# All of f on ScalarE's queue, the chain to the row of sums in two column pieces, and a new order of operations

## The chip, the cores and the metric

The kernel runs on one core of one Trainium2 chip. The metric is device time in microseconds (us), the median of several runs. All times in this document are us unless a unit stands beside them.

## The reference

An attention with a forget gate is followed by a bilinear feed-forward layer. There are 8 batches, 8 heads, 576 positions and 64 columns a head; the layer has 4608 tokens, 512 model columns and 1536 inner columns.

```python
scores = scale * np.matmul(q, k.transpose(0, 1, 3, 2))
log_f = np.log(np.clip(f, 0.0001, 1.0))
cum = np.cumsum(log_f, axis=-1)
decay = cum[:, :, :, None] - cum[:, :, None, :]
scores = np.where(causal, -1000000000.0, scores + decay)
...
attn = attn / (np.sum(attn, axis=-1, keepdims=True) + 1e-09)
x = np.matmul(attn, v)            # then heads side by side: 4608 x 512
out = (x @ w_a) * (x @ w_b) @ w_out
```

`f` has one number for each batch, head and position. In a row of scores the term of the query's own position is the same for all keys and falls out in the softmax, so the kernel needs only the running sum of -log f over the keys.

## The kernel before

**Tiles.** A tile t is a batch b and a pair of heads (t = 4b + pr, 32 tiles). Its 576 queries are cut into five blocks i = 0 to 4 of 128 (the last of 64) and its scores into groups: group 0 holds the blocks 1 and 0, group 1 block 2 (384 keys wide), group 2 block 3, group 3 block 4. A group's scores are made in PSUM by `qk_group` (L390), the row maximum is taken on VectorE (`do_max`, L474, for batch 0; `do_decay`, L500, which also adds the sums, for the others), the exponential on ScalarE (`do_exp`, L531 and L527), the reciprocal of its sum on VectorE (L541, L539), the product with it on GpSimd (`do_norm`, L549). The probabilities are turned either by TensorE (batch 0, `pe_tr`, L569) or by a DMA transpose of the SP queue (`do_tr`, L563), and multiplied with v (`do_pv` L591, `do_pv4` L607). The attention's result lies turned in `xT`. Tiles of batch 0 and 1 have their turned probabilities in the unused second half of `xT` (the tiles `xT0` to `xT3` in a DMA's name), later ones in `PTA` and `PTB`. The feed-forward layer makes `psa` and `psb` (`ff_mm`, L861), copies and multiplies them (L213 on ScalarE, L872 on VectorE, giving `ht`), and makes `pso` (L881).

**The opening.** f is loaded in four DMAs of 32 partitions each: two from ScalarE's queue (`f_load`, `f_rows`, L173), two from GpSimd's. Then comes a chain with one instruction a step over all 576 columns: VectorE clips (L184), ScalarE takes the logarithm (L186), VectorE makes the running sum (L187), its upper half in 16 bits (L189) and, in partitions of its own, the rest (L190). The result is `crow`, 128 partitions of 576 sums in fp16. TensorE adds it to the scores of batch 0 (a matmul `sc<-crow,pick` in `qk_group`) and spreads it over partitions for batch 1 (`spread_mm`, L442, tile `scd`). The sums also go to memory (L195) and come back as `spread` for the later batches (L453). Meanwhile q and k of batch 0 come in by four loads of the SP queue (L243: q, k, and a second half of each, which lies in the tile `wout`), are made fp16 (`cast_qk`, L211 to L217, on any of three engines), turned on TensorE (`pe_transpose`, L258, tile `psT`) and copied to `qT` and `kT` (`pe_evict`). ScalarE loads a table for the logarithm and one for the exponential; `warm_table` (L176) does it ahead of time with one small activation each.

**The order.** Every operation is an `Op` with engines that may do it. Two lists made beforehand, `ORDER` (the numbers of all operations in the order of their issue) and `CHOICE` (a letter for each operation that several engines may do: D VectorE, A ScalarE, P GpSimd), decide everything; `laid_out` reads them. Each engine works strictly in the order in which its instructions were issued, and so do the DMA queues: an instruction that waits holds up all behind it on its engine. The costs and due times in `Op` (durations, `prio`, `land`) served to find the lists and do nothing at run time.

**Buffers.** Two score buffers (`sc`), three of `ff` in PSUM (for `psT`, `scd`, `psP`, `psa`, `psb`, `pso`), one of `pv`.

Of the kernel before, what the change touches and what calls it, by code (L numbers as in the profile page):

```python
# [11 lines left out]
EXP = mybir.ActivationFunctionType.Exp  # L12
# [13 lines left out]
def kernel(  # L26
# [138 lines left out]
    def f_load(_):  # L165
        f_rows(nc.scalar, 0)

    def f_rows(eng, c):
        if not cw:
            f_tiles()  # L170
        rows = f.rearrange("b (h p) s -> h b p s", h=2)
        for half in range(2):
            eng.dma_start(out=cw["f"][64 * half + 32 * c:64 * half + 32 * c + 32, :], in_=rows[half])  # L173

    def warm_table(func):
        return lambda _: nc.scalar.activation(out=warm, in_=warm, func=func)  # L176
# [7 lines left out]
    o1 = Op("DVE", 0.45, lambda _: nc.vector.tensor_scalar(out=cw["f"], in0=cw["f"], scalar1=1e-4,  # L184
                                                           scalar2=1.0, op0=MAX, op1=MIN), [o_f, o_f2], prio=-300)
    o2 = Op("ACT", 0.7, lambda _: nc.scalar.activation(out=cw["l"], in_=cw["f"], func=LN), [o1, o_w], prio=-300)  # L186
    o3 = Op("DVE", 1.35, lambda _: nc.vector.tensor_tensor_scan(  # L187
        out=cw["f"], data0=cw["1"], data1=cw["l"], initial=0.0, op0=MUL, op1=SUB), [o2, o0], prio=-300)
    o4 = Op("DVE", 0.45, lambda _: nc.vector.tensor_copy(out=cw["h"], in_=cw["f"]), [o3], prio=-300)  # L189
    o5 = Op("DVE", 0.75, lambda _: nc.vector.scalar_tensor_tensor(  # L190
        out=crow, in0=cw["h"], scalar=lowrow[:, 0:1], in1=cw["f"], op0=MUL, op1=ADD), [o4, o_c], prio=-300)
# [4 lines left out]

    o6 = Op("SP", 1.1, cum_store, [o3], prio=-300, land=0.4)
    o_e = Op("ACT", 1.4, warm_table(EXP), [o2], prio=-300)
    for u in s_users:
        u.extend([o_f2, o0, o1, o2, o3, o4, o5, o6])  # L200
# [437 lines left out]
    def attention(t, base):  # L638
# [12 lines left out]
        if not direct:  # L651
            if t in PSPREAD:
# [3 lines left out]
                for h in range(2):  # L656
                    bm = Op("PE", 512 * COLS, lambda _, h=h: spread_mm(t, h), [o5, bc0] + bcs, prio=prio(0) - 5, mode="full", name=f"bm{t}")
# [15 lines left out]
        for gs in ([(0,), (1,), (2, 3)] if b in EARLY else [(0, 1), (2, 3)]):  # L673
            deps = [kq_ops[(w, b, pr)] for w in "qk"] + [o_c] + ([o5] if direct else bcs)
# [285 lines left out]
    for n in cuts:  # L960
# [3 lines left out]
        0 1 3 4 19 13 25 31 2 37 20 5 21 6 14 22 7 23 15 26 12 16 260 8 24 11 17 9 54 32 27 18 261 57 28 63 33  # L964
        30 58 262 65 29 59 64 55 263 34 69-71 36 99 264 60 66 35 102 38 39 41 234 10 144 103 108 110 109 104 40
# [3 lines left out]
        56 175 138 220 75 139 81 221 176 183 184 207 87 76-78 241 228 82 229 88 83 242 101 243 118 163 80 79 164  # L969
# [8 lines left out]
        384 385 460 470 301 467 468 289 386 290 296 297 469 291 292 232 1676-1678 479 317 298 1679 374 410 411  # L978
# [4 lines left out]
        1702 1704 420 1703 432 433 428 427 429 1705-1707 421 1708 306 307 1709 399 417 439 440 435 434 1710-1713  # L983
        446 447 441 482 1714 1716 358 1718 1715 442 1719 1720 422 1717 443 489 448 1722-1724 1721 491 498 359
        492 1725 499 505 506 1726 1728 1730 356 1727 493 500 449 357 1729 501 502 436 394 395 400 424 444 431
        430 527 423 445 450 494 490 512 1731 507 508 1732 513 483 488 1733 517 509 484 402 403 655 451 453
        1734-1736 518 495 514 519 520 1739 529 454 1740 531 455 521 532 545 538 539 546 510 438 437 511 497
        503 504 496 522 523 533 1737 1741 1744 1746 408 650 566 452 530 1742 534 1745 540 541 1747 515 516 409
        406 1748 542 535 552 553 547 548 1749-1754 1756 1757 554 537 656 528 536 549 550 544 407 524 1755 557
        1758 1759 485 567 651 551 543 1760-1762 558 555 1763-1765 559 560 1766 1767 657 525 569 1743 608 662 676  # L990
        667 658 1768 659 1769 570 573 1770 1771 456 580 561 457 587 574 581 588 571 652 1772 458 562 556 563-565
        1738 575 653 654 1774 1776 1773 582 576 1777 583 459 1775 1778 572 1780 1779 590 1781 1782 584 577 594
        1783 1784 1786 589 1785 1788-1790 595 1787 596 663 579 568 591 1791 599 600 609 593 585 586 592 668 578
        602 1792-1794 664 1795 601 666 611 615 603 597 598 665 629 616 613 623 617 605 604 660 718 1796 661 677
        719 618 1797-1799 630 622 1800 612 619 1802 625 1803 632 624 631 606 607 674 672 1804 1805 614 636 637
        633 1806 1808 1807 1809 1810 638 1811 610 641 1812 626 1813-1815 642 635 621 634 628 675 620 627 643
# [4 lines left out]
        740 726 1850-1852 741 735 734 728 1853 742 724 746 747 846 760 856 850 761 720 751 752 847 802 848 748  # L1001
        1855-1857 851 717 716 1801 763 753 852 754 861 1854 854 743 729 749 736 1858 730 738 744 737 731 750 767
        769 768 775 770 853 781 755 774 776 777 745 857 757 771 782 765 758 1860-1862 783-785 766 1865 788 789
# [57 lines left out]
        2315 2314 2317 2316 2319 2318 2321 2320 2322 2323 2326 2324 2327 2325 2328 2331 2329 2332-2334 2330 2335  # L1061
# [49 lines left out]
```

## Time and profile before

| | us |
|---|---|
| runs | 417.01, 418.45, 418.51 |
| median | 418.45 |
| the profiled execution | 415.86 |
| its span, first to last instruction | 414.1 |
| TensorE busy | 391.0 (94%) |
| VectorE busy | 301.3 (73%) |
| ScalarE busy | 276.9 (67%) |
| GpSimd busy | 254.7 (62%) |

The profile is of one execution, 1.76 longer than its span and 2.59 below the median of the runs. PE is TensorE, DVE VectorE, ACT ScalarE, POOL GpSimd; "SPq" and "ACTq" are the sequencers that issue DMAs. A row of the timeline has the start, the duration, the engine, the line of the kernel, the tile written and those read, the shapes, and in brackets how long the engine had been idle before and what ended the wait. A matmul's end is modelled and overlaps with the next one's start, so for TensorE the distance of two starts counts.

### The profile page before, as it was taken

The page shows a single profiled execution, that of the slowest core. Times are in us where ns is not written, and L with a number is a line of the kernel's source. Part 1 is how long each engine was busy: PE and PEld are TensorE (multiplying, and loading weights), DVE is VectorE, ACT ScalarE, POOL GpSimd, SP SyncE. Part 2 cuts the span into 40 slices and gives each one's busy share as a digit, 9 for nine tenths or more (in the row PEclk, how much of TensorE's full clock was granted, in tenths as well). Part 3 has the DMA queues.
Part 4 walks back from the last instruction along what each step waited for, and adds up shares of the span by engine and source line. Part 5 has one row for each costly group of instructions (what it writes and reads, how often), then busy time and mean ns, then how long its engine had stood idle before and what let it go on. Part 6 is the DMA issues. An engine that isn't in the chain of part 4 may idle for free.

```text
span 414.1 us, 10945 instructions
## 1 busy us (share of the span) xinstructions
PE 391.0 (94%) x3860; PEld 212.0 (51%) x3860; DVE 301.3 (73%) x1002; ACT 276.9 (67%) x788; POOL 254.7 (62%) x442
## 2 busy tenths in 40 slices
PE   0688999998999999999999999999999999999996
PEld 0445785765755544444444544454444444444552
DVE  2889998996878958867987889678777885342240
ACT  2786899775867797766777687687787583231231
POOL 8699698766876867674886687676675745000000
PEclk9999999998999999999999999999999999999999
DMA  8899799999999999999979999999689727300202
GB/s 272 175 220 258 172 210 228 236 206 268 294 239 218 286 229 192 267 215 281 192 206 249 237 271 220 246 211 244 170 181 221 185 57 145 116 1 2 101 2 77
DMA packets 153528, 80.72 MB, mean 195 GB/s; under 512 B 130784, under 2 KB 133344, under 8 KB 153472
## 3 DMA queue, kind: packets, MB, share of 16 engines
q1 hardware_dynamic: 149536, 75.01, 77.1%
q0 software_dynamic: 3856, 4.87, 7.0%
q8 instruction: 30, 0.49, 0.5%
q14 instruction: 26, 0.21, 0.2%
q10 hardware_dynamic: 80, 0.15, 0.1%
HBM read 52.20 MB, written 9.58 MB: 149 GB/s over the span
## 4 chain that ended last, share of the span: by engine, by line
PE 82%; ACT 5%; DVE 4%; DMA 4%; POOL 2%; issue 1%; SPq 1%; POOLq 0%; DVEq 0%; ACTq 0%
PE psa L861 22%; PE pso L881 21%; PE psb L861 21%; PE sc L390 9%; PE pv L591 5%; ACT PA L531 2%; PE psT L258 2%; DMA wout<-in_k_dram 2%; DVE st L474 1%; DMA xT<-PA 1%; PE psP L569 1%; DVE S L500 1%; ACT PB L531 1%; PE sc L607 1%; SPq L563 1%
## 5 line engine op out<-in xcount | busy, mean ns | idle before, releaser
L500 DVE CUSTOM_DVE_ANT_0 S<-sc,spread 64x576 f32<-64x576 f32 (+4 forms) x232 | 125.3, 561 | 8.3 <-PE sc L390 3.5
L861 PE MATMUL psa<-xT,wa 128*128 128x512 f16 (+2 forms) x528 | 115.8, 342 | 0.9 <-DVE ht L872 0.5
L861 PE MATMUL psb<-xT,wb 128*128 128x512 f16 (+2 forms) x528 | 115.6, 342 | 0.3 <-ACT PTB L213 0.3
L549 POOL TENSOR_SCALAR PA<-PA,st 128x128 f16<-128x128 f16 (+2 forms) x192 | 90.1, 483 | 21.0 <-DVE st L541 13.9
L872 DVE TENSOR_TENSOR ht<-psb,a 128x512 f16<-128x512 f32 (+2 forms) x132 | 77.7, 590 | 34.8 <-PE psb L861 28.3
L213 ACT CAST a<-psa 128x512 f16<-128x512 f32 (+2 forms) x132 | 66.4, 504 | 53.4 <-PE psa L861 46.6
L881 PE MATMUL pso<-wout,ht 128*128 128x512 f16 x432 | 99.0, 382 | 0.4 <-DVE osb L217 0.4
L531 ACT ACTIVATE PA<-S,st 128x256 f16<-128x256 f32 (+2 forms) x168 | 84.2, 505 | 12.6 <-DVE st L500 12.5
L549 POOL TENSOR_SCALAR PB<-PB,st 128x512 f16<-128x512 f16 (+1 forms) x96 | 67.8, 715 | 28.1 <-DVE st L541 12.0
L861 PEld LDWEIGHTS <-wb 128*128 128x128 f16 x528 | 50.8, 98 | 40.8 <-issue 0.4
L861 PEld LDWEIGHTS <-wa 128*128 128x128 f16 x528 | 49.0, 98 | 41.3 <-issue 2.6
L881 PEld LDWEIGHTS <-ht 128*128 128x128 f16 x432 | 40.9, 98 | 47.7 <-issue 1.1
L531 ACT ACTIVATE PB<-S,st 128x512 f16<-128x512 f32 x56 | 40.2, 719 | 13.6 <-DVE st L500 12.4
L390 PE MATMUL sc<-kT,qT 64*128 64x128 f16 (+5 forms) x480 | 43.8, 278 | 3.9 <-ACT PA L531 2.2
L531 ACT ACTIVATION_READ_ACCUMULATOR PA<-S,st 128x1 f32 x168 | 32.3, 192 | 0.0
L390 PEld LDWEIGHTS <-qT 64*128 64x128 f16 (+1 forms) x480 | 17.3, 97 | 26.7 <-issue 20.8
L527 ACT ACTIVATE PB<-S,st 128x576 f16<-128x576 f32 x28 | 21.7, 776 | 12.3 <-issue 5.4
L541 DVE RECIPROCAL st<-st 128x2 f32<-128x2 f32 x128 | 18.7, 157 | 14.6 <-ACT PB L531 8.2
L217 DVE CAST xT<-pv 128x512 f16<-128x512 f32 (+1 forms) x40 | 23.0, 576 | 7.5 <-PE pv L591 7.4
L500 DVE CUSTOM_DVE_ANT_1 S<-sc,spread 128x256 f32<-128x256 f32 x48 | 19.8, 419 | 10.3 <-PE sc L607 8.2
L466 POOL TENSOR_SCALAR_AFFINE_SELECT spread<-spread 128x256 f32<-128x256 f32 x24 | 9.8, 408 | 28.0 <-DVE st L500 27.9
L459 POOL TENSOR_SCALAR_AFFINE_SELECT spread<-spread 128x768 f32<-128x768 f32 x24 | 20.9, 872 | 9.1 <-DMA spread<-cum_d 9.1
(85 smaller groups left out, 418.1 us busy)
## 6 DMA issues: line engine op xcount, KB each, us to landing
spread<-cum_d SPq DMA_DIRECT2D x24, 576.0 KB, 5.8
out_dram<-osb SPq DMA_DIRECT2D x36, 256.0 KB, 3.3
q<-in_q_dram SPq DMA_DIRECT2D x15, 576.0 KB, 5.9
k<-in_k_dram SPq DMA_DIRECT2D x15, 576.0 KB, 5.4
v<-in_v_dram SPq DMA_DIRECT2D x32, 256.0 KB, 4.5
wout<-in_moe_w_out_dram POOLq DMA_DIRECT2D x3, 512.0 KB, 6.6
v<-in_v_dram SPq DMA_DIRECT2D x8, 128.0 KB, 5.1
wa<-in_moe_w_a_dram POOLq DMA_DIRECT2D x2, 512.0 KB, 7.5
```

The source lines that it names most:

```text
L213: nc.scalar.copy(out=out_, in_=in_)
L217: VEC[e].tensor_copy(out=out_, in_=in_)
L390: nc.tensor.matmul(out=dst, lhsT=lhsT, rhs=rhs, start=start, stop=stop, skip_group_check=True)
L459: nc.gpsimd.affine_select(out=c[:, :, 0:SM].rearrange("p h (j k) -> p h j k", k=128), in_=c[:, :, SM:2 * SM].rearrange("p h (j k) -> p h j ...
L500: nc.vector.tensor_tensor_reduce(out=o, in0=x, in1=y, scale=-1.0, scalar=3e38, op0=ADD, op1=MIN, accum_out=m)
L527: nc.scalar.activation(out=p_blocks(t, 4), in_=T[("s" if direct else "z", t, 4)], func=EXP, bias=st[:, 8:9], scale=sign, accum_out=st[:, 1 ...
L531: nc.scalar.activation(out=p_blocks(t, i)[:, :, h, :], in_=(T[("s", t, i)][:, h, :] if direct else T[("z", t, i)][:, h * n:h * n + n]).rea ...
L549: VEC[e].tensor_scalar(out=p, in0=p, scalar1=st[:, c:c + 1], scalar2=1.0, op0=MUL, op1=MUL)
L591: nc.tensor.matmul(out=o[HP[h], 128 * i:128 * i + 128], lhsT=vt[:, j, pr + NP * h, :], rhs=pt[:, base_blk[i] + 2 * block_at(t, i, j) + h, ...
L861: nc.tensor.matmul(out=p[:, 0:n], lhsT=w16[:, db, 128 * fb:128 * fb + 128], rhs=xTflat[db][:, t0:t0 + n], start=(db == 0), stop=(db == 3))
L872: nc.vector.tensor_tensor(out=ht[:, 0:n], in0=T.pop(("psb", t0, fb))[:, 0:n], in1=T.pop(("a16", t0, fb))[:, 0:n], op=MUL)
L881: nc.tensor.matmul(out=o, lhsT=T[("ht", t0, fb)][:, 128 * tb:128 * tb + 128], rhs=wout16[:, fb, :], start=(fb == 0), stop=(fb == 11))
```

## The change

All four loads of f are issued by ScalarE's queue, two after each other for each half of the heads. The chain of five steps is cut into two column pieces, 0 to 256 and 256 to 576, with the running sum of the second carried on from the last column of the first. Group 0 of a tile in batch 0, which needs 256 sums, waits only for the first piece of `crow`; all else waits for both. The table for the exponential is now asked for after both logarithms. All numbers of `ORDER` and 99 letters of `CHOICE` are new.

```diff
     def f_load(_):
-        f_rows(nc.scalar, 0)
-
-    def f_rows(eng, c):
-        if not cw:
-            f_tiles()
         rows = f.rearrange("b (h p) s -> h b p s", h=2)
         for half in range(2):
-            eng.dma_start(out=cw["f"][64 * half + 32 * c:64 * half + 32 * c + 32, :], in_=rows[half])
+            for c in range(2):
+                nc.scalar.dma_start(out=cw["f"][64 * half + 32 * c:64 * half + 32 * c + 32, :], in_=rows[half])
...
-    o_f = Op("ACT", 2.05, f_load, prio=-310, land=0.3)
+    def clip(lo, hi):
+        x = cw["f"][:, lo:hi]
+        nc.vector.tensor_scalar(out=x, in0=x, scalar1=1e-4, scalar2=1.0, op0=MAX, op1=MIN)
+
+    def scan(lo, hi):
+        nc.vector.tensor_tensor_scan(out=cw["f"][:, lo:hi], data0=cw["1"][:, lo:hi], data1=cw["l"][:, lo:hi],
+                                     initial=cw["f"][:, lo - 1:lo] if lo else 0.0, op0=MUL, op1=SUB)
+
+    def low_part(lo, hi):
+        nc.vector.scalar_tensor_tensor(out=crow[:, lo:hi], in0=cw["h"][:, lo:hi], scalar=lowrow[:, 0:1],
+                                       in1=cw["f"][:, lo:hi], op0=MUL, op1=ADD)
...
+    f_tiles()
+    o_f = Op("ACT", 4.05, f_load, prio=-310, land=0.3)
     s_users = [take(o_f, "S") for _ in range(2)]
-    o_f2 = Op("POOL", 1.3, lambda _: f_rows(nc.gpsimd, 1), prio=-310, land=0.3)
...
-    o1 = Op("DVE", 0.45, lambda _: nc.vector.tensor_scalar(out=cw["f"], in0=cw["f"], scalar1=1e-4,
-                                                           scalar2=1.0, op0=MAX, op1=MIN), [o_f, o_f2], prio=-300)
-    o2 = Op("ACT", 0.7, lambda _: nc.scalar.activation(out=cw["l"], in_=cw["f"], func=LN), [o1, o_w], prio=-300)
-    o3 = Op("DVE", 1.35, lambda _: nc.vector.tensor_tensor_scan(
-        out=cw["f"], data0=cw["1"], data1=cw["l"], initial=0.0, op0=MUL, op1=SUB), [o2, o0], prio=-300)
-    o4 = Op("DVE", 0.45, lambda _: nc.vector.tensor_copy(out=cw["h"], in_=cw["f"]), [o3], prio=-300)
-    o5 = Op("DVE", 0.75, lambda _: nc.vector.scalar_tensor_tensor(
-        out=crow, in0=cw["h"], scalar=lowrow[:, 0:1], in1=cw["f"], op0=MUL, op1=ADD), [o4, o_c], prio=-300)
...
+    crow_ops, lns = [], []
+    o3 = None
+    for lo, hi in ((0, 256), (256, S)):
+        n = hi - lo
+        o1 = Op("DVE", 0.06 + 0.00073 * n, lambda _, lo=lo, hi=hi: clip(lo, hi), [o_f], prio=-300, name="fclip")
+        o2 = Op("ACT", 0.2 + 0.00083 * n, lambda _, lo=lo, hi=hi: nc.scalar.activation(
+            out=cw["l"][:, lo:hi], in_=cw["f"][:, lo:hi], func=LN), [o1, o_w], prio=-300, name="fln")
+        o3 = Op("DVE", 0.02 + 0.00232 * n, lambda _, lo=lo, hi=hi: scan(lo, hi), [o2, o0] + ([o3] if lo else []),
+                prio=-300, name="fscan")
+        o4 = Op("DVE", 0.06 + 0.0007 * n, lambda _, lo=lo, hi=hi: nc.vector.tensor_copy(
+            out=cw["h"][:, lo:hi], in_=cw["f"][:, lo:hi]), [o3], prio=-300, name="fhi")
+        o5 = Op("DVE", 0.06 + 0.0013 * n, lambda _, lo=lo, hi=hi: low_part(lo, hi), [o4, o_c], prio=-300, name="flo")
+        crow_ops.append(o5)
+        lns.append(o2)
...
-    o_e = Op("ACT", 1.4, warm_table(EXP), [o2], prio=-300)
+    o_e = Op("ACT", 1.4, warm_table(EXP), lns, prio=-300)
...
-            deps = [kq_ops[(w, b, pr)] for w in "qk"] + [o_c] + ([o5] if direct else bcs)
+            deps = [kq_ops[(w, b, pr)] for w in "qk"] + [o_c] + (crow_ops[:1 if gs == (0,) else 2] if direct else bcs)
...
     ORDER = """
-        0 1 3 4 19 13 25 31 2 37 20 5 21 6 14 22 7 23 15 26 12 16 260 8 24 11 17 9 54 32 27 18 261 57 28 63 33
...
+        23 17 29 35 41 2 24 25 0 1 3 26 18 27 19 4 5 20 21 30 6-9 22 28 36 16 31 45 42 46 264 48 47 49 54 58 32
...
     CHOICE = """
-        DPAAPPADPPADAPDAPDPAAAADDDDADDADDDDDDDDAADAADDDDDAAAAAADAADAAAADAADAAAAAADAAADAAAAADDADAADAAAAAAAAA
+        DDADDDAAAPADDDDDPPPDAADDAAADDDDDDDADADDDADDDADADAAADAAAAADAAADAAADAADAAAAAAAAAAAAAADAAAAAADAADDAAAA
     """
```

What the new lists make of the opening, engine by engine, in the order of issue:

- **ScalarE**: four loads of f; the logarithm's table; a copy to `qT`; logarithm of the first piece; a copy to `kT`; a cast of k's second half; copies to `qT` and `kT`; logarithm of the second piece; the exponential's table; exponentials of the tiles 0 and 1. `warm_table(EXP)` comes after these and loads nothing.
- **VectorE**: the casts of q and k (four instructions), then clip, sum, copy and rest of the first piece; clip of the second; a copy to `kT`; two casts of q's second half; three maxima; the sum of the second piece; a copy to `qT`; copy and rest of the second piece; further maxima. The second of the three maxima waits for ScalarE's first exponential, the columns being in one tile.
- **TensorE**: q and k turned; group 0 of tile 0; k's second half turned; group 0 of tile 1; q's second half turned; group 1 of tile 0; a spread; group 0 of tile 2, and so on.
- **GpSimd**: the constants at once; a cast of half of k's second half; two casts of v; four loads of `wa` and `wb`; then the first products of `do_norm`.
- **SP**: the four loads of q and k as before; v, which now waits for a semaphore of f's first load; the next batch's q and k.

More of the change, by code (lines that the diff above doesn't have):

```diff
@@ L165, in f_load, with cum_store @@
     def f_load(_):
-        f_rows(nc.scalar, 0)
-    def f_rows(eng, c):
-        if not cw:
-            f_tiles()
         rows = f.rearrange("b (h p) s -> h b p s", h=2)
         for half in range(2):
-            eng.dma_start(out=cw["f"][64 * half + 32 * c:64 * half + 32 * c + 32, :], in_=rows[half])
+            for c in range(2):
+                nc.scalar.dma_start(out=cw["f"][64 * half + 32 * c:64 * half + 32 * c + 32, :], in_=rows[half])
     def warm_table(func):
         return lambda _: nc.scalar.activation(out=warm, in_=warm, func=func)
-    o_f = Op("ACT", 2.05, f_load, prio=-310, land=0.3)
+    def clip(lo, hi):
[7 more added lines that the diff above has]
+                                       in1=cw["f"][:, lo:hi], op0=MUL, op1=ADD)
+    def cum_store(_):
+        for half in range(2):
+            nc.sync.dma_start(out=cum_d[:, half * S:half * S + S], in_=cw["f"][64 * half:64 * half + 32, :])
+    f_tiles()
+    o_f = Op("ACT", 4.05, f_load, prio=-310, land=0.3)
     s_users = [take(o_f, "S") for _ in range(2)]
-    o_f2 = Op("POOL", 1.3, lambda _: f_rows(nc.gpsimd, 1), prio=-310, land=0.3)
     o_c = Op("POOL", 4.5, lambda _: constants(), prio=-300)
@@ L183 @@
     o_w = Op("ACT", 2.2, warm_table(LN), [o0], prio=-300)
-    o1 = Op("DVE", 0.45, lambda _: nc.vector.tensor_scalar(out=cw["f"], in0=cw["f"], scalar1=1e-4,
-                                                           scalar2=1.0, op0=MAX, op1=MIN), [o_f, o_f2], prio=-300)
-    o2 = Op("ACT", 0.7, lambda _: nc.scalar.activation(out=cw["l"], in_=cw["f"], func=LN), [o1, o_w], prio=-300)
-    o3 = Op("DVE", 1.35, lambda _: nc.vector.tensor_tensor_scan(
-        out=cw["f"], data0=cw["1"], data1=cw["l"], initial=0.0, op0=MUL, op1=SUB), [o2, o0], prio=-300)
-    o4 = Op("DVE", 0.45, lambda _: nc.vector.tensor_copy(out=cw["h"], in_=cw["f"]), [o3], prio=-300)
-    o5 = Op("DVE", 0.75, lambda _: nc.vector.scalar_tensor_tensor(
-        out=crow, in0=cw["h"], scalar=lowrow[:, 0:1], in1=cw["f"], op0=MUL, op1=ADD), [o4, o_c], prio=-300)
-    def cum_store(_):
-        for half in range(2):
-            nc.sync.dma_start(out=cum_d[:, half * S:half * S + S], in_=cw["f"][64 * half:64 * half + 32, :])
+    crow_ops, lns = [], []
[12 more added lines that the diff above has]
+        lns.append(o2)
+        for u in s_users:
+            u.extend([o0, o1, o2, o3, o4, o5])
     o6 = Op("SP", 1.1, cum_store, [o3], prio=-300, land=0.4)
-    o_e = Op("ACT", 1.4, warm_table(EXP), [o2], prio=-300)
+    o_e = Op("ACT", 1.4, warm_table(EXP), lns, prio=-300)
     for u in s_users:
-        u.extend([o_f2, o0, o1, o2, o3, o4, o5, o6])
+        u.append(o6)
     o_p = Op("POOL", 4.0, lambda _: paddings(), [o_c], prio=-100)
@@ L656, in attention @@
                 for h in range(2):
-                    bm = Op("PE", 512 * COLS, lambda _, h=h: spread_mm(t, h), [o5, bc0] + bcs, prio=prio(0) - 5, mode="full", name=f"bm{t}")
+                    bm = Op("PE", 512 * COLS, lambda _, h=h: spread_mm(t, h), crow_ops + [bc0] + bcs, prio=prio(0) - 5, mode="full", name=f"bm{t}")
                     su = take(bm, "ff")
@@ L984 @@
[L984 to L988, printed above, removed]
@@ new lines @@
+        1689 1739 412 449 507 428 427 455 492 1737 513 514 518 521 522 413 500 501 454 531 523-525 527 515 1740
+        360 533 361 535 536 549 550 519 543 542 508 526 520 457 659 1743 1744 410 411 537 552 1741 538 544 545
+        529 528 1745 458 459 534 1748-1750 1746 556 539 1751 1752 1754 1753 551 1756 1757 557 1755 1758 541 532
+        1759 660 553 1760 1762 1761 1763 561 555 655 571 540 456 1764 1765 558 1766 1767 562 559 546 1768-1774
+        661 1775 564 563 662 663 573 565 574 1776 1777 656-658 460 1778 1780 1782 577 578 591 575 1779 592 461
@@ new lines @@
+        1742 666 548 560 547 566 567 554 1781 579 1784 1786 462 580 584 585 587 1785 586 1783 1787 576 1788 1789
+        612 680 568 569 671 1747 664 1790 598 1791 588 463 599 581 1792 594 1793 593 1794 667 613 681 572 1795
+        600 603 601 595 604 1796-1798 605 1799 606 668 615 607 619 626 633 634 617 616 627 620 669 670 583 589
+        596 582 590 597 602 621 608 609 672 1801-1803 628 636 635 1804 1806 1807 622 629 1808 678 610 611 676
+        618 1810-1812 1809 630 640 641 1814 642 1815 614 1813 1816 637 645 638 665 639 1817-1820 673 646 1821
@@ new lines @@
+        643 631 644 674 647 648 675 683 649 650 1822 1824 1826 687 689 1823 695 623 632 624 694 688 701 1825 625
+        684 685 697 1827 690 691 696 702 1828 1805 722 1800 848 1830 703 1831 1829 1832 1833 698 686 708
+        1834 1835 704 1836 709 1837 677 651-653 723 692 679 693 699 682 1838 1840 1842 710 1839 713 711 1841 714
+        1844 1846 1843 715 716 1847 725 1848 1845 717 705 729 743 1849 707 849 700 719 706 712 718 1850 1852 731
+        1851 744 727 730 736 737 1853 745 738 739 746 732 1854 1855 850 1856 728 851 1857 733 852 750 740 751
@@ new lines @@
+        2194-2196 2199 2200 1582 2201 2197 1583 2204 1627 2193 2198 2202 2205 1628 2206 1629 2207 2203 2208 2209
+        2211 2210 2212 2213 2215 2217 2214 2216 2218-2221 2223 2222 2225 1584 2224 2226 2227 1585 2228-2233 2235
+        2234 2237 2236 2238 2239 2241 2240 2242 2243 2245 2247 2244 2246 2248 2249 1630 2250-2253 2255 2257 2254
+        2256 2258 2259 2262-2264 2267-2269 2265 1631 2260 2261 2266 2272 2270 2273-2275 2271 2277 2279 2278 2281
+        2280 2283 2282 2285 2284 2287 2286 2289 2291 2290 2288 2292 2293 2295 2294 2297 2296 2299 2298 2301 2300
```

86 lines of the change are left out of this document (27 added, 59 removed), and 85 rows, old and new, of the table ORDER.

## The prediction

> **What bounds the kernel now.** I read the page first, then the stages, the chain of waits, and the timeline of the opening and of the one hole later on.
>
> ```profile
> PE   0688999998999999999999999999999999999996
> DVE  2889998996878958867987889678777885342240
> PEclk9999999998999999999999999999999999999999
> ```
>
> TensorE is full from the third slice on (a slice is 10.35). In the steady part it can hardly gain; what is left lies ahead of slice 4, in slice 9, and after the last matmul, where the order of the last rows on every engine stays as it was. The stages say how much:
>
> ```profile
> 0.00:12.90 12.90, 1.73 (x38) 1.15 (x40) 4.65 (x8) 4.78 (x8) 10.90 (x41) 1.00 0.92 262
> 20.00:31.80 11.80, 9.77 (x100) 5.73 (x98) 10.09 (x25) 9.96 (x38) 11.53 (x23) 1.00 1.08 208
> 100.10:400.00 299.90, 298.94 (x2723) 152.96 (x2723) 217.79 (x743) 200.46 (x561) 174.91 (x289) 1.00 0.82 192
> 93.60:95.40 1.80, 0.00 (x0) 0.03 (x1) 0.41 (x2) 1.69 (x6) 1.80 (x5) 1.00 1.22 256
> 96.70:100.10 3.40, 3.40 (x15) 1.50 (x13) 2.03 (x9) 1.31 (x6) 1.09 (x2) 0.50 0.97 308
> ```
>
> The columns are the stretch, its length, then busy time of PE, its weight loads, DVE, ACT and POOL, the granted clock and the DMA's share. Before 12.90 TensorE does 1.73 of work; from 20 to 31.8 it is idle for 2.03; from 100 to 400 for 0.96. After a hole of 1.8 at 93.6 the clock is halved for 3.4, which costs half of that, 1.7: the hole's price is 1.85 + 1.7 = 3.55. It ends here:
>
> ```profile
> 95.44 0.36 PE L591 MATMUL pv<-xT,nv 128*64 128x128 f16 x6 [1.85 <-DMA xT<-PA]
> ```
>
> A DMA transpose of the SP queue, issued at 90.69, landed at 95.40. And the opening:
>
> ```profile
> 8.81 0.73 DVE L184 TENSOR_SCALAR cum_f<-cum_f 128x576 f32<-128x576 f32 x1 [7.24 <-DMA cum_f<-in_f_dram]
> 9.58 0.68 ACT L186 ACTIVATE cum_l<-cum_f 128x576 f32<-128x576 f32 x1 [5.21 <-DVE cum_f L184]
> 10.29 1.36 DVE L187 TENSOR_TENSOR_SCAN cum_f<-cum_f,cum_l 128x576 f32<-128x576 f16 x1
> 10.81 1.28 ACT L176 ACT_TABLE_LOAD   x1
> 12.73 1.28 DVE L190 SCALAR_TENSOR_TENSOR crow<-cum_l,lowrow,cum_f 128x576 f16<-128x576 f16 x1
> 14.82 1.02 DVE L474 TENSOR_REDUCE st<-sc 128x2 f32<-128x512 f32 x2 [0.81 <-PE sc L390]
> ```
>
> f is in at 8.53 (the second GpSimd load), `crow` is done at 14.01, the first maximum starts at 14.82, and the table of the exponential is loaded beside VectorE's sum, where it costs nothing.
>
> **Step 1, when f is in.** The trace gives packets by queue. ScalarE's two loads were issued by 2.12 and 2.84; their packets ran 4.18 to 4.80 and 6.70 to 8.08. SP's loads beside them landed at 4.81 (q), 7.22 (k), 9.24 and 10.90 (the second halves). So a load of f came through with or just behind the SP load of its number, not soon after its own issue. Two loads took 2.02 to issue; four take about 4.05, done by 4.9. If the pattern holds, the fourth lands between 9.7 (right behind the descriptors of SP's fourth load: v's first packet, behind them, ran at 9.23) and 11.8 (0.9 after 10.90, as the second was after 7.22). The other end: as the first, 2.7 after the end of its issue, so 6.9 to 7.6. I take 10.5, since the second load, the only one with a load before it, is the nearest row. The GpSimd loads that go save 1.35 at the head of GpSimd's queue; its constants, done at 7.15 before, end about 5.8, and nobody waits for them.
>
> [...]
>
> **Step 2, the first piece.** Scaled by 256/576: clip 0.33, logarithm 0.30, sum 0.60, copy 0.20 (of 0.459), rest 0.57; 2.0, with 0.28 from landing to clip and four handovers of 0.04 (9.54 to 9.58) 2.45. I take 2.5, since fixed costs don't shrink; if none shrank at all it would be 4.9. `crow`'s first piece stands at 13.0, 1.0 earlier than all of it before.
>
> **Step 3, the second piece.** Its logarithm stands on ScalarE behind a copy to `kT` that needs TensorE to turn k after tile 0's scores; behind it come the table, the first exponential, and, held by that, VectorE's second maximum, which stands ahead of the second sum. From 13.0: scores to maximum 0.8, 18 transposes 0.73, copy 0.65, logarithm 0.38, table 1.28, exponential with its accumulator 0.57: 17.4. Then on VectorE maxima of 0.42 and 0.69, sum 0.75, copy to `qT` 0.75, copy 0.26, rest 0.71, less 0.08 of overlap at each of five handovers: 3.2. `crow` is whole at 20.7 instead of 14.0.
>
> The table took 1.28 and the next activation began at 12.10, 0.01 after it. [...]
>
> **Step 4, what that costs.** Group 1 of tile 0 ran at 15.73; now it runs at 20.7, while group 0 of tile 1 is early (about 15 instead of 18.74). The common mark is the end of the scores of group 1 of all four tiles, 29.06 before. From 20.7 TensorE still has four groups 1 (0.86 each, 28.20 to 29.06), two groups 0 (0.97, 26.15 to 27.12), four spreads (0.55) and two turnings (0.82): 9.2, so 29.9 if it never waits: +0.9. It waited 2.03 in this stretch before; with that, +2.9. VectorE's 23 instructions up to the last of these maxima are 9.9, so 30.6 against 30.13: never below +0.5 with f at 10.5. GpSimd's first product comes near 22 instead of 18.64, but four of its weight loads (2.7) are behind it by then. I take **+1.9**, the middle. After the mark VectorE is busy for 23.65 of 25.1 and TensorE for 24.26, so little of it is made good. With f at 7, VectorE's casts of k hold the clip until about 9.0: 1.7 less.
>
> **Step 5, the hole at 93.6.** By column counts TensorE's queue has 56.1 of work up to the product that waited; in the new order 57.1 up to the product with `xT2`'s second part and 58.3 up to `xT3`'s first. From 62.69 on the SP queue issues without rest, about 1.8 a row. `xT2`'s second part moves back by two rows (issued at 85.78 before, so landing near 90), and one of those is a whole spread load: 94 to 96, against TensorE at 94.6. `xT3` moves back by one row: 97.2 against 95.8. Together a wait of about 1.4 to 2, as now: I take **0**. Ends: -3.55 when all of it goes, +3.55 when it doubles and the clock falls again. The same count for the later transposes gives no tile less lead than the tightest has now (3.0 behind TensorE's count in the old order, 2.9 in the new).
>
> **Step 6, changes of tiling.** TensorE's order changes between its three uses (64 rows, 64 columns, full) 231 times instead of 226. A change costs 0.11:
>
> ```profile
> 154.84 0.97 PE psa L861 x4
> 155.81 0.86 PE psb L861 x4
> ```
>
> **+0.55**; ends 0 and 1.1. Casts that move from GpSimd to VectorE run before 9, where VectorE had waited 7.24; q's second half (two, 1.3 to 1.9) stands in step 3 beside ScalarE's path.
>
> **The sum.** 1.9 + 0 + 0.55 = +2.45. The profiled execution would go from 415.86 to 418.3. The median stands 2.59 above it, and the same kernel's runs spread by 1.5; on the median I forecast **420.9**. A difference under 0.5% (2.1) can't be told from none with this kernel.
>
> **The rivals.**
>
> - *The hole closes* (the other side). TensorE is 1.9 late and the SP queue isn't: then `xT2` and `xT3` are there first. It decides whether the SP rows from `xT0` on start later than 62.69. For it: SP runs there at the DMA's pace. Against: its first transpose needs GpSimd's products, late too. 418.45 + 2.45 - 3.55 = 417.35.
> [...]
> [...]
> - *The hole doubles*, with a second fall of the clock: 424.45. For it: two more rows ahead of `xT2`, and TensorE with only 1.0 more work.
> - *The pieces do nothing*, since each load has all columns and the first piece waits for all four: that is in the sum, where the gain is only 1.0.
>
> **Chances.** Forecast 0.45 (own range 419.0 to 423.0), hole closes 0.19, f early 0.09, hole doubles 0.17, both 0.10. Faster by over 0.5% (below 416.36): "both" and half of "hole closes", 0.20. Slower (above 420.54): six tenths of the forecast, "doubles" and a little of "f early", 0.46. Between: 0.34. All low ends together are -1.2 - 3.55 + 0 = -4.75, all high ends +2.9 + 3.55 + 1.1 = +7.55; I give 413.7 to 426.0.
>
> **What would show it.** [...] Step 2: the first scores' maximum near 14 to 15.6. Step 3: the table load behind the second logarithm, `crow` whole near 20.7. Step 4: the end of the last group 1 near 31. Step 5: TensorE's wait for `xT2` or `xT3` near 95, with the clock at 0.50 behind it. I am wrong if the opening's late second piece is made good before 64, or if a DMA transpose that I count as in time is not.

## The result and the profile after

The changed kernel takes 424.35 (median of four runs, 422.90 to 427.76) against 417.73 for the kernel before in the same comparison: the ratio is 1.0163, with a 95% interval of 1.0129 to 1.0197. That is 6.8 slower. The forecast was 2.45 slower; the direction is right, and 4.4 is missing. The profiled execution, 425.17 long, has a span of 423.4, against 414.1 before. Of these 9.3 about 2.5 is more than the repeated runs show: single executions of one kernel lie up to 4 from its median, so the verdicts below go by the ratios of repeated runs (one per cent is 4.2), and the profiles tell only where the time went.

The slices of the profile after, 10.6 each:

```profile
PE   1378999998999999999899999989999999999996
DVE  2779899995878776877787788778877885342340
PEclk9999999999999999999999999999999999999999
```

TensorE now shows an 8 in slices 20 and 27, from 201 and from 275 on, where before it was full to the end. The stages, with the columns as in the prediction:

```profile
0.00:12.90 12.90, 2.19 (x40) 1.38 (x41) 4.05 (x10) 4.01 (x7) 6.54 (x33) 1.00 0.90 253
20.00:31.80 11.80, 8.28 (x72) 4.61 (x71) 9.12 (x23) 8.67 (x34) 6.04 (x15) 1.00 0.91 154
99.30:101.00 1.70, 0.17 (x6) 0.18 (x8) 0.79 (x7) 1.36 (x4) 1.44 (x3) 1.00 1.16 281
101.00:400.00 299.00, 292.61 (x2672) 148.83 (x2669) 214.11 (x735) 198.51 (x557) 173.98 (x287) 1.00 0.85 195
```

From 101 to 400 TensorE is idle for 6.4, where it was idle for 0.96 from 100 to 400 before. The one hole of 1.85 has become two, of 0.97 before 95.20 and of 1.53 before 100.83, and the clock stays at 1.00 behind both (95.20 to 99.30 and 101 to 400). The opening, from the timeline (line numbers from here on are those of the kernel that a view is of; in the changed one L176 is the clip, L405 `qk_group`, L489 `do_max` and L546 `do_exp`):

```profile
10.69 0.29 DVE L176 TENSOR_SCALAR cum_f<-cum_f 128x256 f32<-128x256 f32 x1 [3.08 <-DMA cum_f<-in_f_dram]
15.72 1.28 ACT L546 ACT_TABLE_LOAD   x1
17.02 0.47 ACT L546 ACTIVATE PA<-sc,st 128x256 f16<-128x256 f32 x1
20.34 0.55 DVE L183 SCALAR_TENSOR_TENSOR crow<-cum_l,lowrow,cum_f 128x320 f16<-128x320 f16 x1
20.81 0.42 DVE L489 TENSOR_REDUCE st<-sc 128x2 f32<-128x256 f32 x1
21.32 0.47 ACT L546 ACTIVATE PA<-sc,st 128x256 f16<-128x256 f32 x1 [2.79 <-DVE st L489]
22.75 0.50 PE L405 MATMUL sc<-kT,qT 64*128 64x384 f16 x2 [6.73 <-ACT PA L546]
```

The clip starts at 10.69 and the row is whole at 20.89; group 1 of tile 0 starts only at 22.75, and what it waited for is an exponential, not the row. And the chain of waits around the longest wait of the later part, start, duration, work:

```profile
192.96 0.45 PE pso L896 x2
...
193.43 0.70 DVE osb L232
...
194.15 0.75 SPq L906
...
194.95 0.44 SPq L468
...
195.49 6.66 DMA PTB<-PB
...
202.19 0.58 PE pv L606 x14
```

Read it from below: TensorE's product waits for a transpose; the transpose was issued late, because on the SP queue an output store (L906) stood ahead of it; the store waited for a copy on VectorE, and that for TensorE's own `pso`. Before the change both transposes of that tile stood ahead of the store; the second of them and the stores on the SP queue of the kernel before:

```profile
189.06 2.87 SPq L563 DMA_TRANSPOSE PTB<-PB  x1
192.02 1.01 SPq L891 DMA_DIRECT2D out_dram<-osb  x2
```

### The profile page after: what moved, and what is told of

Its sections match the earlier page's. It is cut to its first block, busy times and chain, and to the rows that moved or that the text cites. A ratio compares the mean times of both kernels' runs of the same rounds, so it can differ in the third digit from the quotient of the medians.

```text
span 423.4 us, 10937 instructions
## 1 busy us (share of the span) xinstructions
PE 389.6 (92%) x3860; PEld 211.1 (50%) x3860; DVE 301.4 (71%) x1009; ACT 279.1 (66%) x790; POOL 250.7 (59%) x436
## 4 chain that ended last, share of the span: by engine, by line
PE 67%; DMA 10%; DVE 8%; ACT 5%; POOL 5%; issue 3%; SPq 1%; POOLq 0%; ACTq 0%; DVEq 0%
PE psb L876 19%; PE psa L876 19%; PE pso L896 15%; PE sc L405 7%; PE pv L606 4%; ACT PA L546 3%; DMA PTA<-PA 2%; DVE S L515 2%; PE psT L273 2%; POOL PB L564 2%; DVE st L489 2%; POOL PA L564 2%; DMA PTB<-PB 2%; DMA xT<-PA 2%; DMA v<-in_v_dram 1%
## 5 line engine op out<-in xcount | busy, mean ns | idle before, releaser
L515 DVE CUSTOM_DVE_ANT_0 S<-sc,spread 64x576 f32<-64x576 f32 (+4 forms) x232 | 125.4, 561 | 10.5 <-PE sc L405 4.6
L564 POOL TENSOR_SCALAR PA<-PA,st 128x256 f16<-128x256 f16 (+2 forms) x192 | 90.2, 481 | 35.0 <-DVE st L556 22.4
L546 ACT ACTIVATE PA<-S,st 128x256 f16<-128x256 f32 (+2 forms) x168 | 84.2, 504 | 17.6 <-DVE st L515 17.4
L564 POOL TENSOR_SCALAR PB<-PB,st 128x512 f16<-128x512 f16 (+1 forms) x96 | 67.6, 712 | 19.2 <-DVE st L556 10.8
L876 PEld LDWEIGHTS <-wb 128*128 128x128 f16 x528 | 49.9, 98 | 40.9 <-issue 1.4
L405 PE MATMUL sc<-kT,qT 64*128 64x256 f16 (+5 forms) x480 | 43.6, 278 | 12.0 <-ACT PA L546 7.5
L546 ACT ACTIVATE PB<-S,st 128x512 f16<-128x512 f32 x56 | 40.2, 719 | 12.4 <-DVE st L515 10.9
L405 PEld LDWEIGHTS <-qT 64*128 64x128 f16 (+1 forms) x480 | 16.9, 98 | 36.2 <-issue 25.6
L546 ACT ACTIVATION_READ_ACCUMULATOR PA<-S,st 128x1 f32 x168 | 32.1, 191 | 0.0
L228 ACT COPY osb<-pso 128x512 f32<-128x512 f32 x19 | 10.9, 574 | 24.6 <-PE pso L896 14.9
```

Source lines behind the costliest of these rows:

```text
L228: nc.scalar.copy(out=out_, in_=in_)
L405: nc.tensor.matmul(out=dst, lhsT=lhsT, rhs=rhs, start=start, stop=stop, skip_group_check=True)
L515: nc.vector.tensor_tensor_reduce(out=o, in0=x, in1=y, scale=-1.0, scalar=3e38, op0=ADD, op1=MIN, accum_out=m)
L546: nc.scalar.activation(out=p_blocks(t, i)[:, :, h, :], in_=(T[("s", t, i)][:, h, :] if direct else T[("z", t, i)][:, h * n:h * n + n]).rea ...
L564: VEC[e].tensor_scalar(out=p, in0=p, scalar1=st[:, c:c + 1], scalar2=1.0, op0=MUL, op1=MUL)
L876: nc.tensor.matmul(out=p[:, 0:n], lhsT=w16[:, db, 128 * fb:128 * fb + 128], rhs=xTflat[db][:, t0:t0 + n], start=(db == 0), stop=(db == 3))
```

## The experiments

Each kernel was timed in five rounds beside the kernel before. **Theory A** was formed from the two traces: the opening costs 2 to 3, and the new order of the later part costs about 4 by itself. **Theory B**: only the opening counts, and makes all that follows late. **Theory C**: the loads on ScalarE's queue are the cost. An order is cut at a point where the old and the new one have issued the same operations, or nearly so; "old order" means the numbers and letters of the kernel before, carried over to the new numbering. Of the 99 letters of `CHOICE` 42 differ between the two kernels, 7 of them behind 195. No experiment parts the order from the letters that go with it.

**1. The loads alone**, in the kernel before.

```diff
-    o_f2 = Op("POOL", 1.3, lambda _: f_rows(nc.gpsimd, 1), prio=-310, land=0.3)
+    o_f2 = Op("ACT", 1.95, lambda _: f_rows(nc.scalar, 1), prio=-310, land=0.3)
```

> The kernel before, with its own order and its chain in one piece; only the two loads of f of GpSimd's queue are issued by ScalarE's queue instead. In the changed kernel the clip began at 10.69 instead of 8.81. Theory A (the opening costs about 2.7, the new order of the steady part costs about 4 by itself): clip near 10.7, the row of sums about 1.9 later than 14.01, total +0.5 to +2 over the kernel before. Theory B (only the late opening counts, and it makes everything later by a chain of late transfers): the same here or more, +2 to +4. Theory C (the loads on ScalarE's queue are the main cost): +4 or more.

Ratio 1.0052 (1.0024 to 1.0080), +2.2. The clip starts at 10.54 and `crow` is done at 16.17 instead of 14.01. Theory C is out. The total is just above theory A's range and inside theory B's, so it doesn't part these two.

**2. Loads and pieces, all in the old order.** In `ORDER` each single step became its two pieces:

```diff
-        5 6 7 8 9
+        4 9 5 10 6 11 7 12 8 13
```

> The changed kernel's code, loads and two pieces alike, with the order and choices of the kernel before: each single step of the chain is replaced by its two pieces after each other, and the exponential's table comes where it stood. Theory A: within 0.7 of the kernel with the loads alone, so +0.5 to +2.5 over before. Theory B: like theory A if the end of the first group 1 scores is less than 2 late, more otherwise. Theory C: +4 or more.

1.0063 (1.0039 to 1.0088), +2.6. With the order left alone, the code of the change costs 2.6, of which the pieces are 0.4 (no more than noise). This again is just above theory A's range, and B allows it too.

**3 and 4. The new order up to about 50, then the old one, and the reverse.**

> The changed kernel with its own order and choices for the first 230 operations (to about 50 us), and the order of the kernel before for all that is left. Theory A: the opening's share alone, +2.5 to +3.5. Theory B: the whole loss, +6 to +7, since the opening is as late as in the changed kernel. Theory C says nothing more than that it is not below the kernel with old order and two pieces.

> The reverse: the changed kernel's code with the order of the kernel before up to the same point (three of the feed-forward layer's first blocks, about 50 us), and the changed kernel's own order for all that is left. Theory A: about 4 above the kernel with two pieces and all of the old order, so +4.5 to +6 over before. Theory B: equal to that kernel within 1, so +0.5 to +2.5.

1.0134 (1.0106 to 1.0162), +5.6, and 1.0180 (1.0149 to 1.0210), +7.5. The 5.6 lies between the two theories' ranges and the 7.5 above both, and together the two kernels would lose more than the change itself. The third kernel has a wait of TensorE of 2.65 just at the seam (50.45), the fourth one of 0.75 (51.13): the two orders differ by a few operations there, so these two decide nothing about the shares. They speak for a cost of the later order: the fourth is 4.9 above experiment 2.

**5. Three output stores back behind the transposes or loads they had overtaken** (of tiles 9, 13 and 16). The SP queue at the third of them:

```diff
 L578 DmaTransposeAnt PTA<-PA 128x12x128
-L906 DMACopy out_dram<-osb 128x512
 L468 DMACopy spread_83<-cum_d 128x2x576
 L578 DmaTransposeAnt PTB<-PB_80 128x13x128
+L906 DMACopy out_dram<-osb 128x512
```

> The changed kernel with three output stores moved on the SP queue to where they stood before the change: behind the two DMA transposes of tile 9 (so that the load of k's second half for batch 3 is no longer behind the store), behind the transpose of tile 13's first part, and behind that of tile 16's second part. A store waits for TensorE's product and its copy, and what is queued behind it waits too. Theory A (the new order of the later part costs about 4, and these stores are most of it): TensorE's waits of 0.57, 0.70 and 1.81 near 122, 167 and 202 go, total 2 to 3 below the changed kernel. Rival (the transposes are late anyway, by GpSimd's products or by the queue's length): the waits come back elsewhere, total within 0.8 of the changed kernel.

1.0110 (1.0076 to 1.0143), +4.6, so 2.2 below the change; the two intervals put that between about 0.2 and 4.2. The wait near 167 is gone and that near 202 is down to 0.20. That for scores near 122 gave way to one of 0.79 for `pso`, and those near 142 and 281 are longer than in the change (1.58 and 1.63).

**6. The second piece earlier.** VectorE and ScalarE in order of issue:

```diff
 VectorE: maximum, tile 0, block 1
+VectorE: sum, copy and rest of the second piece
 VectorE: maximum, tile 0, block 0        (waits for the first exponential)
 VectorE: maximum, tile 1, block 1
-VectorE: sum of the second piece
 VectorE: copy to qT
-VectorE: copy and rest of the second piece
 VectorE: maximum, tile 1, block 0
...
 ScalarE: exponential, tile 0, block 1, head 0
 ScalarE: exponential, tile 0, block 0, head 0
+ScalarE: exponentials, tile 0, head 1, blocks 1 and 0
 ScalarE: exponential, tile 1, block 1, head 0
-ScalarE: exponentials, tile 0, head 1, blocks 1 and 0
```

> The changed kernel with its opening's order edited: the second piece's sum, copy and rest on VectorE ahead of the second maximum, and tile 0's two remaining exponentials ahead of tile 1's first on ScalarE. Theory A (the opening is lost where the second piece stands behind the exponential, and where the score buffer of tile 0 is freed late): the row of sums whole near 17.5 instead of 20.89, group 1 of tile 0 at 19.8 instead of 22.75, first block of the feed-forward layer 1 to 2 earlier, total 1 to 2.5 below the changed kernel. Rival (what is gained there is lost before 60, since VectorE is nearly full): total within 0.7 of the changed kernel.

1.0062 (1.0040 to 1.0085), +2.6: 4.2 below the change, more than was expected. Its timeline:

```profile
16.89 0.55 DVE L183 SCALAR_TENSOR_TENSOR crow<-cum_l,lowrow,cum_f 128x320 f16<-128x320 f16 x1
19.12 0.51 PE L405 MATMUL sc<-kT,qT 64*128 64x384 f16 x2 [3.47 <-ACT PA L546]
```

The row is whole at 17.44 and group 1 of tile 0 starts 3.6 earlier; the first `psa` starts at 37.33 instead of 41.05. A second sum and two exponentials in another place are worth as much as the whole later part.

**7. The pieces alone, with the loads and the order of before.**

> The two pieces alone: f loaded by ScalarE's and GpSimd's queues as before the change, the order and choices of the kernel before, with the chain in two pieces, the first one finished before the second one's sum. The clip stays near 8.8, the first piece of the row is ready near 11 to 12, the whole row near 14. If the pieces are worth something by themselves: tile 0's first maximum near 14.0 instead of 14.82, total -1 to -0.3 against the kernel before. If the row was not what the start waited for: within 0.7 either way. If the five further instructions on VectorE cost: +0.5 to +1.5.

1.0016 (0.9995 to 1.0037): no gain can be seen, and no loss beyond 1.6.

**8. Edits 5 and 6 together.**

> The changed kernel with both edits, the three stores and the second piece. Theory A: the sum of the two gains, 3 to 5 below the changed kernel, so +1.5 to +3.5 above the kernel before. Rival (each order of the later part fits only the opening that it was made for): less than the better one of the two edits gains by itself.

1.0040 (1.0018 to 1.0062), +1.7. Below both edits, and 5.1 below the change, of 6.4 if the gains added up. The 0.9 that the three stores gain beside edit 6 is within the noise.

**9 to 12. Where the later part loses.** Edit 6 with the old order from about 105 on; the same with old loads; the change itself with the old order from 105 on; edit 6 with the old order from 195 on.

The list at the seam of the third, behind operation 690 of 2340 (the other three are cut alike; the last behind 1220):

```diff
         571 540 456 1764 1765 558
-        1766 1767 562 559 546 1768 1769 1770
+        546 554 548 547 1766 562 559 1767
...
```

> The kernel with the second piece earlier (same opening edits), its own order up to 29 of the feed-forward layer's 132 first blocks (690 operations, about 105), and the order and choices of the kernel before for all that is left. In its profile that kernel was 1.0 ahead of the kernel before at 56 and 3.7 ahead at 107, and then lost 6.7. Theory A (the new order of the later part, from 107 on, has the loss in itself): about 4 below the kernel with the second piece earlier, -2 to -0.5 against the kernel before. Rival D (the queue of transposes is the bound up to 113 in both, so what a late hole saves comes back as waits near 110): +0.5 to +2 over the kernel before. Rival (the later part fits only its own start): no gain against the kernel with the second piece earlier, +2.6.

> As the last, with two of f's loads back on GpSimd's queue. The clip near 9 instead of 10.4; tile 0's group 0 waits for its turned k until 12, so the first maximum comes 0.6 to 1 earlier. Theory (f's landing is what the two pieces wait for): 0.5 to 1.5 below the last kernel. Rival (TensorE's and ScalarE's copies of k and q are as late): within 0.4 of it.

> The changed kernel's own order up to the same 690 operations (about 108 there), and the order of the kernel before for all that is left. Theory A: the stage from there on costs about 4 in the new order, so about +2.5 over the kernel before instead of +6.6. Rival (what counts is how late the opening is): +5 or more, as in the kernel with the new opening and the old rest.

> As the first of these four, with the seam later: the new order up to 60 of the 132 first blocks (1220 operations, about 195), then the order of the kernel before. It tells where the later part loses. If between 105 and 195 (TensorE's waits of 0.83 and 1.91 at 116 and 138): within 1.5 of the kernel with the second piece earlier, +1.5 to +2.6 over before. If behind 195 (1.37 at 196, 1.26 at 356): -0.5 to +1.

The four results:

- 9: 0.9996 (0.9973 to 1.0020), 2.8 below edit 6, between the ranges of theory A and of rival D.
- 10: 1.0004 (0.9977 to 1.0030), no different from 9, as its rival had it: an earlier f gains nothing here.
- 11: 1.0080 (1.0050 to 1.0110), 3.5 below the change. It missed its +2.5 by 0.8, but lies on the side of theory A.
- 12: 0.9972 (0.9948 to 0.9997), 3.8 below edit 6, more than either case allowed.

The later order's loss lies behind 195, against the waits at 116 and 138 that I had suspected.

**13 to 16. The later order by itself.** The kernel before with the new order only behind 195; edit 6 with the old order behind 195 and the old loads; the change with the old order behind 195; edit 6 with the third store of experiment 5 alone.

> The kernel before, with its own loads, chain and order up to 60 of the 132 first blocks (about 195), and only behind that the order and choices of the changed kernel. Up to the seam the same operations have been issued in both. Theory A (that order costs 3 to 4 by itself): +3 to +4 over the kernel before, with waits of TensorE near 200 (for a transpose behind an output store), and near 280 or 355. Rival (it costs only behind a changed opening): within 1 of the kernel before.

> The second piece earlier, the order of the kernel before from 195 on, and two of f's loads back on GpSimd's queue. Theory (an earlier f is worth something here): 0.5 to 1.5 below the same kernel with all loads on ScalarE's queue, so -2.7 to -1.7 against the kernel before. Rival (as at the earlier seam, where the old loads gained nothing): -1.5 to -0.5.

> The changed kernel with its own order up to 195 and the order of the kernel before behind it. Theory A: 3 to 4 below the changed kernel, +2.5 to +3.8 over the kernel before. Rival: within 1.5 of the changed kernel, +5 or more.

> The kernel with the second piece earlier, and of the three stores only the one behind tile 16's transposes moved. If that store is the larger part of what is lost behind 195: 1.3 to 2.5 below the kernel with the second piece earlier, +0.1 to +1.3 over the kernel before. If the loss is spread over many small waits: within 0.8 of it, +1.8 to +3.4.

The seam of the first, in the numbers of the kernel before:

```diff
         917 907 934 908 909 920
-        1041 921 935 1042 1918-1921
+        1048 1918-1920 921 1041 1042 936
...
```

- 13: 1.0097 (1.0067 to 1.0128), **+4.1 in the kernel before, with nothing else of the change**.
- 14: 0.9967 (0.9939 to 0.9995), no different from 12, again as the rival had it.
- 15: 1.0062 (1.0038 to 1.0085), 4.2 below the change.
- 16: 1.0026 (1.0000 to 1.0051), 1.5 below edit 6; the two intervals put that between about 0.1 and 2.9.

Theory A stands in three independent pairs (experiments 12 and 6, 13 and the kernel before, 15 and the change: 3.8, 4.1 and 4.2, each good to 1.3 to 1.8). Stage by stage, first in the kernel before, then in experiment 13; the columns are as above:

```profile
195.00:240.00 45.00, 45.00 (x456) 22.44 (x453) 37.05 (x126) 32.40 (x94) 33.06 (x55) 1.00 0.95 233
240.00:280.00 40.00, 39.97 (x370) 19.26 (x369) 32.27 (x118) 30.94 (x88) 29.87 (x50) 1.00 1.02 230
280.00:320.00 40.00, 40.00 (x368) 19.42 (x368) 32.17 (x118) 30.53 (x89) 25.52 (x44) 1.00 0.84 203
320.00:360.00 40.00, 40.00 (x306) 18.88 (x303) 27.12 (x85) 21.55 (x60) 19.13 (x34) 1.00 0.58 135
```

```profile
195.00:240.00 45.00, 44.71 (x433) 21.86 (x430) 34.72 (x123) 34.69 (x98) 29.58 (x49) 1.00 0.99 239
240.00:280.00 40.00, 39.06 (x396) 19.30 (x391) 32.24 (x114) 28.39 (x84) 29.39 (x48) 1.00 0.89 217
280.00:320.00 40.00, 39.53 (x364) 19.46 (x363) 32.16 (x117) 28.14 (x79) 27.31 (x47) 1.00 0.93 215
320.00:360.00 40.00, 38.58 (x291) 18.02 (x290) 26.90 (x90) 23.94 (x69) 19.16 (x36) 1.00 0.59 122
```

Where the old order leaves TensorE no idle time but 0.03, the new one leaves 0.3, 0.9, 0.5 and 1.4: 3.1 in these two executions, for the 4.1 of the repeated runs. Four of its waits from there:

```profile
196.47 0.25 PE L591 MATMUL pv<-PTB,nv 128*64 128x128 f16 x2 [0.29 <-DMA PTB<-PB]
278.33 0.44 PE L258 MATMUL psT<-ident,q 64*128 64x64 f16 x18 [0.77 <-POOL q L215]
285.58 0.36 PE L591 MATMUL pv<-PTA,nv 128*64 128x128 f16 x6 [0.47 <-DMA PTA<-PA]
358.15 0.25 PE L591 MATMUL pv<-PTB,nv 128*64 128x128 f16 x2 [1.00 <-DMA PTB<-PB]
```

Three are for transposes, 1.8 in all. Only the first goes back to an output store that was queued ahead of the transpose. In the chain of waits the one at 278 goes back over GpSimd's cast of q to the load of q, which stood on the SP queue behind a store and two transposes and was issued at 271.50 (at 269.33 in the kernel before). The one at 358 goes back to a transpose that waited until 352.84 for GpSimd's last product, with no store ahead of it. The wait behind the one store is 0.29 in this execution, 1.37 in that of experiment 6 and 1.81 in the change: its size differs from kernel to kernel, but it is there each time.

## Why the prediction was wrong

- **Step 1, when f is in: right.** The clip began at 10.69 for 10.8 forecast (f in at 10.5, and 0.28 from there to the clip), and at 10.29 to 10.80 in experiments 1, 6, 8, 9, 11 and 12, which have the same loads. The pattern behind the forecast held only in part: f's last load was in by 10.69, ahead of SP's fourth (issued at 2.43, landed 9.0 later, at 11.4), not with or behind it. "f early" and "both" in the chances stand for f in at 7 and the clip at 9.0, which none of these runs shows. By themselves the loads cost 2.2 in the old order (experiment 1); the prediction had no price for them alone.
- **Steps 2 and 3: right.** The first piece stands at 13.09 for 13.0, the whole row at 20.89 for 20.7. But the first maximum, which was to gain by the early piece, started at 14.64, only 0.18 earlier than before: VectorE made a copy to `kT` and two casts of q ahead of it. The table load took 1.28 and the next activation began 0.02 after it (17.02), so step 3's sum, which has 1.28 for it, holds there.
- **Step 4: wrong in its mechanism, and too small.** I let group 1 of tile 0 start with the row, at 20.7. It started at 22.75, 1.9 after the row was whole: it needs a score buffer, tile 0's buffer was held by two exponentials, these were queued on ScalarE behind tile 1's, and that waited for tile 1's second maximum at 20.81, behind the second piece. The last group 1 ended at 33.01, 3.95 later than before; the forecast of +1.9 and its end of +2.9 were both too small. By the 33rd matmul of `psa` (59.26 against 56.47) it was 2.8. The 1.0 saved at the hole (next point) made up for most of what the term of 1.9 was short of that, so it is partly luck that the sum of this part comes near. In repeated runs, with the old order behind 195, all of the change up to there costs 2.6 (experiment 15), and so does its code in the old order (experiment 2).
- **Step 5, the hole near 95: right** to 1. TensorE waited 0.97 (for a `PTB`, which the step had not named) and 1.53 (for `xT`) there instead of 1.85, and the clock did not fall, so about 1.0 was saved. The prediction had no way to tell whether it would fall (last section).
- **Step 5, the later transposes: this is the step that failed.** "The same count for the later transposes gives no tile less lead than the tightest has now", I wrote, and put nothing on all that follows the hole. The count added up the SP queue's issue times against TensorE's work, as if the queue never waited. It waits (in the kernel before it issues nothing from 184.71 to 187.53): a store stands in it until TensorE's product has been copied (in the changed kernel the copy ends at 194.13 and the store is issued at 194.15), and a transpose until GpSimd has made its probabilities (in the kernel before the product into `PA` ends at 187.50 and the transpose of `PA` is issued at 187.53). The lead of a transpose is then set by what it and its neighbours in the queue wait for. Measured: +4.1 (experiment 13) for the order behind 195, of which the one store ahead of tile 16's second transpose is about 1.5 (experiment 16). For the rest the place is shown, not the one cause.
- **Step 6, tiling**: 0.55 was not tested by itself. What TensorE's idle time leaves of the 4.1 behind 195, about 1, has room for it; that is no proof.
- **The sum**: 2.6 for the loads, the pieces and the new order up to 195, and 4.1 for the order behind it make 6.7 for 6.8 measured. The forecast of 2.45 was the first part alone.
- **The range** reached 426.0, but by the wrong rivals: the hole that doubles did not occur, and a loss in the steady part was in none of them. That its 424.45 lies next to the measured median is chance.

Open: why f's earlier landing is worth about 2 in the old order (2.2 by experiment 1, 1.9 between experiments 2 and 7) and nothing that can be measured once the second piece is mended (experiments 9 and 10, 12 and 14 differ by 0.1 or less of a per cent), though the first `psa` is 1.9 to 2.0 earlier in these profiles. Open too is how much of the 4.1 is order and how much the 7 letters that go with it; that was not tried.

The two mended versions (experiments 12 and 14) are 0.28% and 0.33% faster than the kernel before, with intervals that end at 0.03% and 0.05%: ahead of the kernel before by little more than can be told apart.

## What to carry to other kernels

A new order for the whole program is a change in every stage: look for each queue at which waiting instruction now stands ahead of which, not only at the sum of durations. On the SP queue here an instruction that waits for a compute engine (a store of results) belonged behind the transposes and loads that the same engine soon needed: one such store moved back was worth about 1.5 (experiment 16). And when a step is late, ask which buffers are held by what is queued behind it: here the first group 1 waited 1.9 more for a buffer when its data was there.

## What the hardware did unexpectedly

The clock. In the kernel before, the trace's record of the clock begins at 31.83; the halved stretch begins at 96.68, is 3.413 long, and starts 19 such lengths behind 31.83. In the changed kernel the record begins at 32.96 and a fall behind the last instruction of TensorE, at 422.08, lies 114 such lengths behind it. In experiment 1 the halved stretches begin at 70.24 and 111.20, in experiment 3 at 50.20 and 115.05, which is 12 and 19 such lengths apart. So in these four executions the falls lie on one grid each. The window of the grid ahead of a fall, and others that were followed by none (the columns are stretch, length, TensorE's busy time, clock, DMA share and GB/s):

```profile
93.27:96.68 3.41, 1.56 (x21) 1.00 1.27 240
```

That is the kernel before, with 1.56 busy; it fell. The changed kernel:

```profile
200.21:203.62 3.41, 1.60 (x34) 1.00 1.12 303
97.81:101.22 3.41, 1.88 (x21) 1.00 1.13 325
```

It did not fall, after 1.60 either. And experiment 7, where a hole of 1.89, longer than the one before the change, ended at 96.52 and lay across two windows:

```profile
92.07:95.49 3.42, 2.55 (x20) 1.00 0.90 228
```

It did not fall there, but at 109.14, after a window with 1.56 from two short waits. Over the seven falls ahead of the programs' ends the window ahead had 1.02 to 1.79 of busy time: 1.56 before the change, 1.34 and 1.73 in experiment 1, 1.02 and 1.65 in experiment 3, 1.56 in experiment 7 and 1.79 in experiment 9. Of the windows without a fall behind the opening, the changed kernel's had 1.60 at the least, and one of experiment 16, whose clock was 1.00 throughout, had 1.68. The two ranges overlap, so no sharp limit shows in this measure (matmul ends are modelled). A hole of 1.85 within one window was followed by a fall, and one of 1.89 across two was not: the prediction's price of 3.55 for a hole of 1.85 was a price of where that one lay.

The opening. Its rows print a clock of 1.00, but the trace's record of the clock begins only at 32.96 (31.83 in the kernel before), and the matmuls say otherwise. Six matmuls of the same shape each, in the changed kernel:

```profile
31.16 0.82 PE L584 MATMUL psP<-ident,PA 128*128 128x128 f16 x6
32.94 0.51 PE L584 MATMUL psP<-ident,PA 128*128 128x128 f16 x6
```

In the changed kernel two `psP` matmuls start up to 0.107 apart ahead of 32.96 and 0.056 behind it, so the same matmul took 1.9 times as long there; that this was about half the clock is an estimate from these two distances. The prices of TensorE's work in step 4 were read ahead of 31.83 in the kernel before (the groups between 26.15 and 29.06), and so fit a stretch that is still slow.
